# Scores of a retention layer in quarters of the TensorE array instead of row halves

## The chip, the core and the metric

The kernel runs on one core of a Trainium2 chip. TensorE does the matrix products, VectorE and ScalarE take their results out of PSUM and do the element-wise work, GpSimd one small scaling, and SyncE issues the DMA transfers. The metric is the device time of one execution in microseconds (us). A time that is compared is the median of several executions; the profile is of one more execution, whose own time is given beside it.

## The reference

A linear attention with decay is run over 768 tokens of 4 sequences with 8 heads of 64 dimensions; its output, seen as 3072 rows of 512, goes through a layer with a leaky ReLU of slope 0.01.

```python
# q, k, v: (4, 8, 768, 64) float32;  w_in: (512, 2048), w_out: (2048, 512)
gamma = 1.0 - 2.0 ** (-5.0 - np.arange(H))
for t in range(S):
    state = gamma * state + k[:, :, t] (outer) v[:, :, t]        # per batch and head, 64x64
    y[:, :, t] = (1 / np.sqrt(D)) * q[:, :, t] @ state
x = y.transpose(0, 2, 1, 3).reshape(B * S, H * D)                # (3072, 512)
h = x @ w_in
out = np.maximum(0.01 * h, h) @ w_out
```

All values are float32 in the result; the weights come in as 64-bit words and are turned into float32 on the chip.

## The kernel before

The 768 tokens are cut into 6 chunks (`c`) of 128 tokens (`C`). In each chunk every sequence (`b`, 4 of them) has its 8 heads held as 4 pairs (`a`, `HP = 4`) of two heads (`j`): a pair's 64 + 64 dimensions fill the 128 partitions. For one chunk and sequence the work is:

- `score` (lines 158 to 165): for each pair `a` and each head `j`, keys against queries. The 64 dimensions of head `j` lie on partitions 64j to 64j+63, so a product uses 64 rows of the array (row half `j`) and all 128 columns. The weights loaded are 128 key tokens, the moving operand 128 query tokens; the 128x128 result lies on all 128 partitions of PSUM. Results of head `j = 0` go to one bank, of `j = 1` to another (tile `ap`, two banks, two buffers under the tag `att`). Eight products.
- `masked` (line 169): VectorE multiplies the eight 128x128 blocks by a triangular mask, out of PSUM into the tile `am`, in one instruction.
- `reads` (line 183): the state of earlier chunks, 64x64 a head, against the queries. Weights of 64 rows (row half `j`) and 64 columns; the result goes to partitions 64i to 64i+63 (column half `i`), so that four products of a group lie in the four quarters of the array. Eight products, from chunk 1 on. Tile `yp`.
- `values` (line 192): masked scores times values: 128 rows, 64 columns (column half `i`), 128 moving columns; eight products onto the same tile `yp`.
- `state` (line 207): keys times values for the next chunk's state: 128 rows, 64 columns, 64 moving columns; eight products, from every chunk but the last.
- `taken` (lines 231 to 234): VectorE scales the result into `x` and renews the state.

The layer behind it takes `x` in chunks too. Its products are done in a scheme with seven block products instead of eight (`seven`, line 388, tiles A to D with the endings `_h` for the first and `_o` for the second matrix), or directly (`direct`, line 410, tile `d`) while the first weights are still being turned into float32; all these use the full array of 128x128 with 256 moving columns. One fp32 product is two records, a weight load and a matmul each, in the trace.

The order on each engine is the order in which the program is written; nothing reorders it. In the first stage (chunks 0 and 1, up to about 54 us) `score` is called for one sequence at a time, eight times, between steps of `direct` and, at the very start, between products that only keep the array busy (line 600). In the chunks 2 to 5 it is called for two sequences in a row, as the functions that `scored` returns: two such pairs of calls a chunk, placed after a given step of `seven` by the lists `at`, and the matching `read` (with `reads`, `values`, `state` and `taken`) three steps later. So in the span there are 24 calls of `score`: 8 alone and 8 pairs.

Of the kernel before, what the change touches and what calls it, by code (L numbers as in the profile page):

```python
# [23 lines left out]
def kernel(  # L24
# [35 lines left out]
    nc = tc.nc  # L60
# [94 lines left out]
    def two_banks(name):  # L155
        return psum.tile([128, 2, HP, C], FP32, tag="att", bufs=2, name=name)

    def score(c, b):

        x = heads[c, b][0]  # L160
        ps = scores[c, b] = two_banks(f"ap_{c}_{b}")
        for a in range(HP):
            for j in range(2):
                nc.tensor.matmul(ps[:, j, a, :], lhsT=x[ts(j, 64), 1, a, :],  # L164
                                 rhs=x[ts(j, 64), 0, a, :])

    def masked(c, b):
        am = work.tile([128, 2, HP, C], FP32, tag="am", bufs=2, name=f"am_{c}_{b}")
# [367 lines left out]
    def scored(c, b):  # L536
        def do():
            decay_v(c, b)
            score(c, b)
            masked(c, b)  # L540
        return do
# [48 lines left out]
    x, t = xs[0]  # L590
# [11 lines left out]

    keep_busy(7)
    score(0, 0)
    masked(0, 0)
    decay_v(0, 0)
    next_powers()
    keep_busy(8)
    score(0, 1)
    masked(0, 1)  # L610
    decay_v(0, 1)
# [209 lines left out]
```

## Time and profile before

| what | value |
|---|---|
| time, median of 4 executions | 672.12 us (672.08 to 672.36) |
| the profiled execution | 672.35 us |
| its span (first to last instruction) | 670.3 us |
| granted TensorE clock in it | 0.999 |
| products of `score` (line 164), matmul records | 304 + 48 + 32 = 384, by the tile that they read |
| the same as busy time | 20.9 + 3.5 + 2.3 us |
| products of `reads` (line 183), matmul records | 272 + 48 = 320; busy 9.5 + 1.8 us |
| VectorE's mask (line 169) | 24 instructions, 28.6 us busy |
| instruction queue | 32 packets, 0.52 MB |

A page of the profile gives busy time by engine, the span in 40 slices, the chain of work that ended last, and groups of instructions. Busy time of TensorE counts a record from its start to its modelled end, and records overlap, so it is not what a group costs; the start of the next record is the better measure. In the chain of waits every piece is the time from one release to the next, so its pieces add up to the span.

### The profile page before, as it was taken

The page shows a single profiled execution, that of the slowest core. Times are in us where ns is not written, and L with a number is a line of the kernel's source. Part 1 is how long each engine was busy: PE and PEld are TensorE (multiplying, and loading weights), DVE is VectorE, ACT ScalarE, POOL GpSimd, SP SyncE. Part 2 cuts the span into 40 slices and gives each one's busy share as a digit, 9 for nine tenths or more (in the row PEclk, how much of TensorE's full clock was granted, in tenths as well). Part 3 has the DMA queues.
Part 4 walks back from the last instruction along what each step waited for, and adds up shares of the span by engine and source line. Part 5 has one row for each costly group of instructions (what it writes and reads, how often), then busy time and mean ns, then how long its engine had stood idle before and what let it go on. Part 6 is the DMA issues. An engine that isn't in the chain of part 4 may idle for free.

```text
span 670.3 us, 9653 instructions
## 1 busy us (share of the span) xinstructions
PE 663.9 (99%) x4132; PEld 577.2 (86%) x4133; DVE 369.8 (55%) x563; ACT 174.2 (26%) x319; POOL 20.2 (3%) x23
## 2 busy tenths in 40 slices
PE   8999999999999999999999999999999999999997
PEld 4888888888888888888888888888888888888886
DVE  4778769889889675414642623553531444341342
ACT  4754456355252002210301210210211220221210
POOL 1000000000000111000000100100100000000000
PEclk9999999999999999999999999999999999999999
DMA  8922221222422553002002200301300000000001
GB/s 325 403 75 95 66 91 64 94 95 63 158 64 63 190 189 126 1 1 100 27 16 79 95 1 1 126 0 64 126 1 0 2 0 31 33 1 1 0 1 63
DMA packets 16025, 49.11 MB, mean 73 GB/s; under 512 B 1904, under 2 KB 2160, under 8 KB 15984
## 3 DMA queue, kind: packets, MB, share of 16 engines
q1 hardware_dynamic: 15984, 48.51, 20.6%
q8 instruction: 32, 0.52, 0.3%
q14 instruction: 9, 0.07, 0.0%
HBM read 42.21 MB, written 6.29 MB: 72 GB/s over the span
## 4 chain that ended last, share of the span: by engine, by line
PE 97%; DMA 1%; DVE 0%; issue 0%; SPq 0%; DVEq 0%
PE A_o L388 12%; PE B_o L388 12%; PE C_o L388 12%; PE B_h L388 12%; PE C_h L388 12%; PE A_h L388 11%; PE D_o L388 6%; PE D_h L388 6%; PE d L410 4%; PE ap L164 4%; PE yp L192 3%; PE yp L183 2%; PE yp L207 1%; DMA qk<-in_qk_dram 1%; PE sums L207 0%
## 5 line engine op out<-in xcount | busy, mean ns | idle before, releaser
L388 PE MATMUL A_h<-x,w 128*128 128x256 f32 x352 | 83.2, 379 | 0.0
L388 PEld LDWEIGHTS A_h<-x,w 128*128 128x128 f32 x352 | 66.9, 190 | 9.0
L388 PE MATMUL A_o<-g,w 128*128 128x256 f32 x288 | 68.0, 379 | 0.0
L423 ACT ACTIVATE g<-g 128x512 f32<-128x512 f32 x66 | 40.1, 630 | 87.0 <-DVE g L337 87.0
L388 PEld LDWEIGHTS A_o<-g,w 128*128 128x128 f32 x288 | 54.8, 190 | 7.4
L428 ACT COPY m<-A_h 128x512 f32<-128x512 f32 x22 | 12.8, 582 | 140.3 <-PE A_h L388 100.5
L337 DVE TENSOR_TENSOR m<-m,B_o 128x512 f32<-128x512 f32 x16 | 10.9, 684 | 65.9 <-PE B_o L388 65.9
L337 DVE TENSOR_TENSOR m<-m,B_h 128x512 f32<-128x512 f32 x22 | 15.1, 685 | 56.2 <-PE B_h L388 56.2
L231 DVE TENSOR_TENSOR x<-yp,dec 128x512 f32<-128x512 f32 x24 | 16.4, 687 | 47.7 <-PE yp L207 35.4
L388 PE MATMUL C_h<-t,w 128*128 128x256 f32 x176 | 42.2, 383 | 0.0
L388 PE MATMUL B_h<-x,w 128*128 128x256 f32 x176 | 42.2, 383 | 0.0
L388 PE MATMUL B_h<-t,w 128*128 128x256 f32 x176 | 41.6, 379 | 0.0
L388 PE MATMUL C_h<-x,w 128*128 128x256 f32 x176 | 41.6, 379 | 0.0
L388 PE MATMUL D_h<-t,w 128*128 128x256 f32 x176 | 41.6, 379 | 0.0
L340 DVE TENSOR_TENSOR gd<-g,gd 128x512 f32<-128x512 f32 x48 | 36.9, 769 | 1.8
L169 DVE TENSOR_TENSOR am<-ap,mask 128x1024 f32<-128x1024 f32 x24 | 28.6, 1220 | 16.2 <-PE ap L164 16.2
L388 PEld LDWEIGHTS C_h<-x,w 128*128 128x128 f32 x176 | 33.5, 190 | 4.5
L388 PEld LDWEIGHTS B_h<-t,w 128*128 128x128 f32 x176 | 33.5, 190 | 4.5
L388 PEld LDWEIGHTS D_h<-t,w 128*128 128x128 f32 x176 | 33.5, 190 | 4.5
L388 PEld LDWEIGHTS C_h<-t,w 128*128 128x128 f32 x176 | 33.0, 190 | 4.9
L388 PEld LDWEIGHTS B_h<-x,w 128*128 128x128 f32 x176 | 33.0, 190 | 4.8 <-issue 0.3
L388 PE MATMUL C_o<-g,w 128*128 128x256 f32 x144 | 34.0, 379 | 0.0
(109 smaller groups left out, 1046.2 us busy)
## 6 DMA issues: line engine op xcount, KB each, us to landing
raw<-in_weights_dram SPq DMA_DIRECT2D x31, 512.0 KB, 4.1
qk<-in_qk_dram SPq DMA_DIRECT2D x19, 512.0 KB, 4.1
kv<-in_kv_dram SPq DMA_DIRECT2D x17, 512.0 KB, 4.7
out_dram<-o SPq DMA_DIRECT2D x23, 256.0 KB, 2.1
in<-in_qk_dram SPq DMA_DIRECT2D x3, 512.0 KB, 7.3
in<-in_kv_dram SPq DMA_DIRECT2D x3, 512.0 KB, 7.8
kv<-in_kv_dram SPq DMA_DIRECT2D x4, 256.0 KB, 7.5
o_in<-in_qk_dram SPq DMA_DIRECT2D x2, 512.0 KB, 8.4
```

The lines of the kernel that those rows point to most:

```text
L164: nc.tensor.matmul(ps[:, j, a, :], lhsT=x[ts(j, 64), 1, a, :], rhs=x[ts(j, 64), 0, a, :])
L169: nc.vector.tensor_tensor(out=am.rearrange("p j a t -> p (j a) t"), in0=scores[c, b].rearrange("p j a t -> p (j a) t"), in1=mask.unsqueeze ...
L183: nc.tensor.matmul(ps[ts(i, 64), j, m, :], lhsT=st[b][ts(j, 64), a, :], rhs=x[ts(j, 64), 0, a, :], start=(m == 0), stop=False, skip_group_ ...
L192: nc.tensor.matmul(ps[ts(i, 64), j, m, :], lhsT=y[:, 1, 2 * a + j, :], rhs=am[:, j, a, :], start=(c == 0 and m == 0), stop=True, skip_grou ...
L207: nc.tensor.matmul(sp[ts(j, 64), a, :], lhsT=y[:, 0, 2 * a + j, :], rhs=y[:, 1, 2 * a + j, :], start=start, stop=True, skip_group_check=True)
L231: nc.vector.tensor_tensor(out=blocks, in0=ps[:, :, 0 : HP // 2, :], in1=gq, op=ALU.mult)
L337: nc.vector.tensor_tensor(out=out, in0=a, in1=b, op=ALU.add)
L340: nc.vector.tensor_tensor(out=out, in0=a, in1=b, op=ALU.subtract)
L388: nc.tensor.matmul(half, lhsT=block(w, sa)[:, k, ts(i, 128)], rhs=rhs[:, k, :], start=(first and (i == 0 or split) and n == 0 and k == 0), ...
L410: nc.tensor.matmul(banks[r][:, i, :], lhsT=block(2 * u, r + 2 * kh)[:, k, ts(i, 128)], rhs=x[:, 2 * kh + th, k, :], start=(step == 0 and i ...
L423: nc.scalar.activation(g[:, i], g[:, i], AF.Prelu, alpha=0.01)
L428: nc.scalar.copy(out=got["m1"], in_=ps)
```

## The change

Each product of `score` is made as two. The 128 key tokens that were loaded as one set of 128 columns are loaded as two sets of 64 columns (`u`); the results of the first set go to partitions 0 to 63 of PSUM, of the second to 64 to 127. The moving operand, the 128 query tokens of head `j`, is the same for both. The order is: for each pair `a`, for each column half `u`, for each row half `j`. The values that arrive in `ap` and their places are the same, and nothing else in the program is changed.

```diff
         for a in range(HP):
-            for j in range(2):
-                nc.tensor.matmul(ps[:, j, a, :], lhsT=x[ts(j, 64), 1, a, :],
-                                 rhs=x[ts(j, 64), 0, a, :])
+            for u in range(2):
+                for j in range(2):
+                    nc.tensor.matmul(ps[ts(u, 64), j, a, :], lhsT=x[ts(j, 64), 1, a, ts(u, 64)],
+                                     rhs=x[ts(j, 64), 0, a, :])
```

One call of `score` is 16 products instead of 8.

## The prediction

> **What bounds the kernel now.** I read the page's first part first, then its chain of waits, because the chain says where a saved microsecond can be collected.
>
> ```profile
> span 670.3 us, 9653 instructions
> PE 663.9 (99%) x4132; PEld 577.2 (86%) x4133; DVE 369.8 (55%) x563; ACT 174.2 (26%) x319; POOL 20.2 (3%) x23
> PEclk9999999999999999999999999999999999999999
> PE 97%; DMA 1%; DVE 0%; issue 0%; SPq 0%; DVEq 0%
> ```
>
> TensorE is busy 99% of the span at the full granted clock, and 97% of the chain that ended last is its own. No other engine or transfer holds it for long, so whatever a score block (the products of `score`, line 164) gains or loses on TensorE is gained or lost by the kernel, except before 14.85 us, where the chain runs over a transfer and VectorE. The second view is that chain in order of time, here between 0 and 63 us (start, length, what; x16 counts records, of which an fp32 product has two).
>
> ```profile
> 2.18 6.76 DMA qk<-in_qk_dram
> 8.98 1.19 PE ap L164 x16
> 13.52 1.29 DVE x L231 x2
> 16.85 1.09 PE ap L164 x16
> ...
> 36.62 1.03 PE yp L183 x32
> 37.66 1.90 PE yp L192 x32
> 39.55 0.93 PE yp L207 x32
> 40.49 1.92 PE d L410 x8
> 42.41 1.09 PE ap L164 x16
> ```
>
> Of the whole span the same view has eight pieces like this one, two blocks back to back:
>
> ```profile
> 302.66 1.99 PE ap L164 x32
> 304.64 1.92 PE C_h L388 x8
> ```
>
> The third view is the rows of the two tiles, with shapes (rows*columns of the array, then the moving operand):
>
> ```profile
> L164 PE MATMUL ap<-qk x304: 271/272/580, 4.5 to 521.8; 64*128 64x128 f32 x152
> L183 PE MATMUL yp<-qk,states x272: 268/269/322, 50.6 to 528.2; 64*64 64x128 f32 x136
> L192 PE MATMUL yp<-am,kv x304: 272/273/325, 10.9 to 530.1; 128*64 128x128 f32 x152
> ```
>
> The reader is to see that line 183, the state reads, already has the form the scores get: 64 rows by 64 columns, 128 moving columns, all four quarters. Its block of 16 products (32 records) takes 1.03 us; a score block of 8 products over full width (16 records) takes 1.09 us. The durations of about 270 ns overlap; the cost is the spacing of the starts.
>
> **The change, part by part.** Starts of single records, read from the trace, split these blocks. Score before: two records (one per row half) start together, and the next two follow 111.6 ns later; the first step is 101 ns longer, and from the last start to the next line's first is 201 ns. One block: 1091 ns; two back to back (16 steps): 1985 ns. State reads: four records start within 21 ns, the next four follow 109 ns later; the first step is 162 ns, the last start to the next line 199 ns; 1034 ns for 16 products.
>
> *A score block alone.* It goes from 8 products to 16 of exactly the state reads' shape, count and quarters: 1091 becomes 1034, -57 ns. There are eight such blocks, all before 46.5 us. The first, at 4.5 us, lies before the transfer that lands at 8.94 us and gains nothing. The second, at 8.98 us, releases VectorE's mask, which leads to the product at 14.85 us. The other six are on TensorE's own chain: at those places VectorE and ScalarE are ahead of TensorE by 0.2 us or more (the closest: the row of x that ends at 21.67 us ahead of a product at 21.91 us), and the saving so far is 0.17 us there. 7 x 57 = 399 ns. If that cover were gone, at most these 0.4 us would be lost.
>
> *Two blocks back to back.* From the third chunk on there are 8 such pairs. Each becomes 64 records, 16 steps of four: 1034 + 8 x 109 = 1906 against 1985, -79 ns; 8 x 79 = 632 ns.
>
> *Entering and leaving.* Entering costs the same for both forms (last start of the line before to the first of the block: 309 ns into line 164 and into line 183, where an unbroken stream has 216). Leaving a quarter form for the full array is not in the trace. Leaving it for 128*64 takes 199 ns, leaving 64*128 for the full array 201, leaving 128*64 with 64 moving columns for the full array 151: in each the last step plus about 92 ns. So I take 199, and 321 ns to the second full-array record, as now. Bounds: at best 103 ns, as where two lines of one form meet (192 to 207), at worst one more such 92 ns; per block -0.10 or +0.09 us, times 15.
>
> *The supply of instructions.* 24 x 8 = 192 more products are 384 more weight loads and 384 more matmul records, 768 on TensorE's stream. The instruction queue's row has 0.52 MB at 0.3% of the DMA engines for 9653 instructions; 8% more of that hides under transfers that are idle for most of the second half. How fast TensorE takes them is another matter: the state reads show 4 records per 109 ns for 32 records, not for the 64 of a pair. Nearest rows: 27 ns a record (the state reads' steps), and 40 ns, the longest dense stretch that the trace has (96 records of lines 183, 192 and 207 in 3.86 us). I take the 27 ns, since that row has the same form and no stall in it; the other end is a rival below.
>
> *The column halves.* In line 183 the two products on one row half read different moving columns; now they read the same ones. No row shows this. Below, nothing; above, no overlap of the two halves, the second rival. I take nothing: reading 512 bytes apart on the same partitions is free in line 183. The order also changes rows before columns, where line 183 changes columns first; its four start within 21 ns, so I give that no price.
>
> *VectorE, ScalarE, GpSimd, SyncE.* The same instructions in the same order. The mask (line 169) waits for the block's last product, which comes some 55 to 75 ns earlier; it waited 16.2 us in all, and its results are used at a later step of the same stage, so only the block at 8.98 us turns that into time. No wait is added.
>
> Sum: -0.40 - 0.63 = -1.0 us. Made against the profiled execution (span 670.3 us, 672.35 us in all, so 2.05 us around it) that is 671.3; against the median of the four runs, 672.12, it is **671.1 us**. With the early cover gone, 671.5.
>
> One rule speaks against the change. The state reads' weight loads of the second step start 53 ns after the first and under the running products: the first step lasts 162 ns, later ones 109, so they are hidden, although both quarters of a row half share rows. The Trainium skill, "TensorE: Matmul & The Clock Gate", section "Part 3: Packing small matmuls — row/col tiling", says weight loads overlap running matmuls only when the row groups differ. By that rule every step of four would be as long as the first, 8 x 162 + 92 = 1.39 us a block and 2.68 us a pair, and the sum +7.7 us; by the row it is the -1.0 us above. The measured steps contradict the rule for quarters, so I go by the row.
>
> **The rivals.** *(A) The pair outruns its supply.* Slower. Place: the second half of each of the 8 pairs, after the 32 records whose pace the trace shows. At 40 ns a record a pair takes 64 x 40.2 = 2.57 us, +0.59; 8 of them +4.7, less 0.4 from the single blocks: **676.4 us**. It decides from 31.8 ns a record on, where a pair costs (1985 + 50) / 64 and eats the single blocks' gain. For it: no stretch of 64 records here is that dense (lines 183 and 192 together take 2.83 us). Against it: the 40 ns are made by steps of two in line 192, and line 207's last records still come every 28 ns.
>
> The same page's table gives TensorE an engine queue of 64, and a state-read block is 64 instructions (loads counted); no run shows whether more than a queueful holds the pace.
>
> *(B) Only two quarters go at a time*, because both column halves read one moving operand or because of the order: the change doesn't do what it says. Steps of two: 16 x 111.6 + 200 = 1986 ns a block, 32 x 111.6 + 200 = 3771 a pair; 7 x 0.90 + 8 x 1.79 = +20.6: **692.7 us**. For it: no row has the shared operand. Against it: line 183's four starts within 21 ns.
>
> *(C) Leaving the quarters is cheap*: 103 instead of 199 ns, 15 times, -1.5 us more: **669.6 us**. For it: only that the pairing isn't in the trace. Against it: the 92 ns at every change of form in it.
>
> **How the numbers follow.** The forecast, -1.0 us, 0.66; A 0.12; B 0.12; C 0.10. The forecast's own range is 670.9 to 671.7 (all of the gain a little larger, or the early part gone and steps of 111 ns). C and B together are 0.22, so the range ends just above C's figure and at A's: 670.6 to 676.4. A change of 0.2% is 1.34 us, about what a measurement of this kernel can tell from none. Within it: nearly all of the forecast (0.62) and A just past its threshold (0.02), 0.64. Faster: C and the forecast's lower edge (0.04), 0.14. Slower: the rest of A (0.10) and B, 0.22.
>
> **What would show it.** Line 164 with 64*64 and 768 records; pieces of 1.03 us x32 and 1.91 us x64 in the chain; four starts, then 109 ns; 199 ns to the next line and 321 after; VectorE's rows as before. A pair above 2.03 us is A; four starts spread over two steps are B; a single block below 0.95 us is C. Wrong altogether if TensorE waits somewhere for VectorE that it didn't wait for before.

## The result and the profile after

The changed kernel takes 671.08 us (median of 42 runs, 670.37 to 671.66) against 672.10 us (60 runs, 671.46 to 672.56): a ratio of 0.9985 with a 95% interval of 0.9980 to 0.9989. That is 1.0 us less, 0.15%. The whole interval lies below 1, so the kernel is faster by a little: between 0.1 and 0.2%.

The page of the changed kernel (every line below 161 has moved down by one):

```profile
span 669.0 us, 10421 instructions
PE 662.7 (99%) x4516; PEld 575.2 (86%) x4517; DVE 367.8 (55%) x563; ACT 174.2 (26%) x319; POOL 22.8 (3%) x23
...
PEclk9999999999999999999999999999999999999999
...
q8 instruction: 35, 0.57, 0.4%
...
PE 98%; DMA 1%; DVE 0%; issue 0%; SPq 0%; DVEq 0%
```

TensorE has 384 more matmul records and as many more weight loads, and is still the whole chain. The instruction queue took three more packets. The rows of the tile `ap` show the new form, and in their last lines the mask's wait:

```profile
L165 PE MATMUL ap<-qk x608: 268/269/473, 4.5 to 520.4; 64*64 64x128 f32 x152
...
L165 PE MATMUL ap<-in x96: 268/269/321, 30.0 to 42.5; 64*64 64x128 f32 x96
...
L165 PE MATMUL ap<-o_in x64: 268/269/321, 16.4 to 21.2; 64*64 64x128 f32 x64
...
who waited for it (us, times):
  DVE am L170: 15.6, 12
```

The chain of waits in order of time (start, length, what), at the places shown before:

```profile
2.17 6.34 DMA qk<-in_qk_dram
...
8.55 1.15 PE ap L165 x32
...
13.10 1.29 DVE x L232 x2
...
16.43 1.04 PE ap L165 x32
...
35.97 1.03 PE yp L184 x32
37.01 1.90 PE yp L193 x32
38.90 0.93 PE yp L208 x32
39.84 1.92 PE d L411 x8
41.76 1.03 PE ap L165 x32
```

and, of the whole span, at one of the eight pairs:

```profile
301.66 1.91 PE ap L165 x64
303.57 1.93 PE C_h L389 x8
```

A score block now costs what a state-read block costs, 1.03 us, and a pair of them 1.91 us instead of 1.99. The pieces around them have kept their lengths. By the single starts, the 57 ns of a block are made of three things: its first step is 53 ns shorter (160 instead of 213), its six later steps are 14 ns shorter together, and its last start comes 13 ns later within its step, as four records take 20 ns to start where two took 7; the 2 or 3 ns left are in the leaving and in rounding.

The first line of the chain is another matter: in this execution the second transfer of queries and keys took 6.34 us instead of 6.76, and the first direct product stands 0.42 us earlier. That is a transfer's luck: the same kernel profiled once more (a1 below) had 6.92 us there, and in eight kernels profiled later (a1, e1, e2, e3, e7 to e10), which issue the same transfers there, the second score block began anywhere from 8.59 to 9.26 us. So the spans (670.3 and 669.0 us) differ by more than the medians do.

The second block's own saving does not reach the first direct product. From that block's start to that product's it is 5.88 us before and 5.88 after. The chain's piece for the block is shorter (1.19 to 1.15 us), and VectorE's first instruction on a piece of weights behind the mask is longer by as much. Two lines of the timeline before,

```profile
9.76 2.04 POOL L147 TENSOR_TENSOR kv<-kv,dec 128x512 f32<-128x512 f32 x2 [8.32 <-DMA kv<-in_kv_dram]
11.33 0.75 DVE L329 TENSOR_SCALAR w<-raw 128x512 uint32<-128x512 uint32 x1
```

and after:

```profile
9.33 2.04 POOL L147 TENSOR_TENSOR kv<-kv,dec 128x512 f32<-128x512 f32 x2 [7.90 <-DMA kv<-in_kv_dram]
10.87 0.79 DVE L330 TENSOR_SCALAR w<-raw 128x512 uint32<-128x512 uint32 x1
```

VectorE's instruction takes 0.75 and 0.79 us here, against 0.41 and 0.42 us the next time, when GpSimd is idle (14.72 and 14.29 us), and it ends 0.28 us after GpSimd has scaled the values, however early it began (0.28 to 0.29 us in ten of the thirteen profiles). In these ten (all but e4, e5 and e6, whose blocks are much longer) the first direct product starts 5.10 to 5.11 us after GpSimd's first scaling does, whatever form the second score block has: in e3 that block starts 0.04 us later than in the changed kernel's first profile, GpSimd 0.20 and the first direct product 0.21 us later. GpSimd starts when its transfer lands. So GpSimd and its transfer set the time there, and not the score block. Why VectorE's instruction is held until then the traces do not show.

For these reasons the experiments below are read by two figures from the trace: the length of a block, from its first record's start to the start of the next line's first record, and the *ledger*, from the first direct product (14.85 us before, 14.43 us after) to the last matmul's start. In the kernel before the ledger is 651.750 us; after the change it is 650.785, 0.965 us less.

### The profile page after: what moved, and what is told of

It reads as the page before. It is cut to its first block, busy times and chain, and to the rows that moved or that the text cites. A ratio compares the mean times of both kernels' runs of the same rounds, so it can differ in the third digit from the quotient of the medians.

```text
span 669.0 us, 10421 instructions
## 1 busy us (share of the span) xinstructions
PE 662.7 (99%) x4516; PEld 575.2 (86%) x4517; DVE 367.8 (55%) x563; ACT 174.2 (26%) x319; POOL 22.8 (3%) x23
## 4 chain that ended last, share of the span: by engine, by line
PE 98%; DMA 1%; DVE 0%; issue 0%; SPq 0%; DVEq 0%
PE A_o L389 12%; PE B_o L389 12%; PE C_o L389 12%; PE C_h L389 12%; PE B_h L389 12%; PE A_h L389 11%; PE D_o L389 6%; PE D_h L389 6%; PE d L411 4%; PE ap L165 3%; PE yp L193 3%; PE yp L184 2%; PE yp L208 1%; DMA qk<-in_qk_dram 1%; PE sums L208 0%
## 5 line engine op out<-in xcount | busy, mean ns | idle before, releaser
L147 POOL TENSOR_TENSOR kv<-kv,dec 128x512 f32<-128x512 f32 x18 | 22.3, 1243 | 460.8 <-DMA kv<-in_kv_dram 251.4
L170 DVE TENSOR_TENSOR am<-ap,mask 128x1024 f32<-128x1024 f32 x24 | 28.6, 1220 | 15.6 <-PE ap L165 15.6
L341 DVE TENSOR_TENSOR gd<-g,gd 128x512 f32<-128x512 f32 x48 | 34.0, 709 | 1.8
```

Of the source, the lines that this page charges most:

```text
L147: engine.tensor_tensor(out=v, in0=v, in1=gk.unsqueeze(2).to_broadcast([128, H, D]), op=ALU.mult)
L170: nc.vector.tensor_tensor(out=am.rearrange("p j a t -> p (j a) t"), in0=scores[c, b].rearrange("p j a t -> p (j a) t"), in1=mask.unsqueeze ...
L341: nc.vector.tensor_tensor(out=out, in0=a, in1=b, op=ALU.subtract)
```

## The experiments

| kernel | one block, ns | a pair, ns | ledger against the kernel before, us | the same from the blocks, us |
|---|---|---|---|---|
| before | 1091 | 1985 | 0 | |
| changed, first and second profile | 1034, 1034 | 1908, 1907 | -0.965, -0.964 | 6 x -57 + 8 x -77.5 = -0.962 |
| e1, pairs alone | 1092 | 1908 | -0.616 | 8 x -77.5 = -0.620 |
| e2, single blocks alone | 1034 | 1985 | -0.342 | 6 x -57 = -0.342 |
| e3, columns first | 1034 | 1908 | -0.962 | 6 x -57 + 8 x -77 = -0.96 |
| e4, sorted by quarter | 2494 | 4468 | +28.275 | 6 x 1403 + 8 x 2483 = +28.28 |
| e5, form changing inside | 1602 | 3203 | +12.807 | 6 x 511 + 8 x 1218 = +12.81 |
| e6, everything twice | 1907 | 3654 | +18.251 | 6 x 816 + 8 x 1669 = +18.25 |
| e7, eighths | 1086 | 1959 | -0.238 | 6 x -5 + 8 x -26 = -0.24 |
| e9, two of a quarter in a row | 1098 | 2058 | +0.620 | 6 x 7 + 8 x 73 = +0.63 |

The last two columns agree within 0.02 us in every row: after the first direct product nothing but the length of the blocks moves the time, even when the blocks become 28 us longer in all.

**Where the microsecond is: the pairs (e1) and the single blocks (e2).** Two kernels with quarters in one of the two places; this edit and those that follow are against the changed kernel:

```diff
         for a in range(HP):
-            for u in range(2):
+            if c > 1:
+                for u in range(2):
+                    for j in range(2):
+                        nc.tensor.matmul(ps[ts(u, 64), j, a, :], lhsT=x[ts(j, 64), 1, a, ts(u, 64)],
+                                         rhs=x[ts(j, 64), 0, a, :])
+            else:
                 for j in range(2):
-                    nc.tensor.matmul(ps[ts(u, 64), j, a, :], lhsT=x[ts(j, 64), 1, a, ts(u, 64)],
+                    nc.tensor.matmul(ps[:, j, a, :], lhsT=x[ts(j, 64), 1, a, :],
                                      rhs=x[ts(j, 64), 0, a, :])
```

In e2 the condition is `c < 2` in place of `c > 1`.

> Quarters in the eight pairs of score blocks alone (chunks 2 to 5); the eight single blocks stay in row halves. Theory (a block is worth what its steps say, wherever it stands): pairs of 1908 ns, singles of 1091 ns, 8 x 78 = 0.62 us below the kernel before, 671.5 us. Rival (what the pairs save is lost again at a later wait): 672.1 us.

> Quarters in the eight single blocks alone (chunks 0 and 1). Theory: singles of 1034 ns, pairs of 1985 ns, 6 x 57 ns on TensorE's own chain and up to 57 ns for the second block, so 0.34 to 0.40 us below the kernel before, 671.7 us. Rival (the first stage is set by transfers and VectorE, so nothing is gained there): 672.1 us.

Measured: 671.81 us (ratio 0.9993, 0.9984 to 1.0002) and 671.92 us (0.9993, 0.9984 to 1.0001), beside 672.38 us for the kernel before on the same chip. The intervals alone can't tell either from no change; the ledgers can, -0.616 and -0.342 us, and they add up to -0.958, beside the -0.965 of both. The rivals fall: nothing is lost again at a later wait, and the six single blocks behind the first direct product count in full.

**The order of the quarters (e3).**

```diff
-            for u in range(2):
-                for j in range(2):
+            for j in range(2):
+                for u in range(2):
```

> The changed kernel with the order of the four quarters turned: the two column halves of a row half come first, as in line 183. Theory (the order of four neighbours does not matter): blocks of 1034 and pairs of 1908 ns, 671.1 us. Rival (rows before columns is a better or a worse order): steps of four other than 109 ns; each ns is worth 8 x 7 + 16 x 8 = 184 ns of the whole.

Measured: 671.40 us (0.9985, 0.9976 to 0.9994), the median block and pair the same to the nanosecond. The order of four neighbours doesn't matter.

**A long stretch (e6).** Each block is computed twice over.

```diff
+        for _ in range(2):
             for a in range(HP):
                 for u in range(2):
                     for j in range(2):
...
```

(The lines inside the new loop are indented further and otherwise as they were.)

> Each score block is computed twice over, into the same place: 32 products a block, 128 records in a row in a pair. Theory (the pace of 109 ns for four records holds as long as one likes): blocks of 1906 ns and pairs of 3653 ns, 7 x 0.87 + 8 x 1.745 = 20 us over the changed kernel, 691 us, up to 1 us more where the mask comes too late for its products in the first stage. Rival (the instructions of a long stretch run short): steps above 109 ns from some record on; at the 40 ns a record of the longest stretch in the kernel before, 5.1 us a pair, 703 us.

Measured: 691.49 us in one run, beside 672.28 for the kernel before. A pair in the chain of waits of this kernel:

```profile
369.71 3.65 PE ap L166 x128
```

The starts of its 128 records go in steps of four, 109 ns apart, to the last (160, 269, 378 ... 3326, 3435 ns). The theory predicted 3653 ns and it is 3654. So rival (A) of the prediction, that a long stretch outruns its instructions, is wrong up to 128 records (256 instructions with the weight loads), twice what a pair needs. The 0.9 us by which the run exceeds the ledger lie before the first direct product (15.75 instead of 14.85 us), where longer blocks delay the mask.

**Does it need neighbours in different quarters (e4, e9)?** First all four products of a quarter in a row, then two:

```diff
-        for a in range(HP):
-            for u in range(2):
-                for j in range(2):
+        for u in range(2):
+            for j in range(2):
+                for a in range(HP):
```

```diff
-        for a in range(HP):
-            for u in range(2):
-                for j in range(2):
+        for m in range(HP // 2):
+            for u in range(2):
+                for j in range(2):
+                    for a in (2 * m, 2 * m + 1):
```

> The changed kernel with its products sorted by quarter: the four products of one quarter in a row, then the next quarter's, so that neighbours in the program cannot go together. Theory (each quarter has a queue of its own, filled far enough ahead): still eight steps of 109 ns a block, 671.1 us. Rival (only neighbours overlap): one quarter at a time, 32 records of 107 ns, 3.4 us a block and 6.9 us a pair, 7 x 2.4 + 8 x 4.9 = 56 us more, 727 us. A look-ahead of some length lies between.

> The changed kernel with two products of one quarter in a row before the next quarter's. Sorting by whole quarters let a quarter begin when the one before it started its fifth record of eight. Theory (a quarter takes four records, one running and three waiting, and only the fifth holds up what is behind it): two products are four records, so nothing is held up, blocks of 1034 ns, steps of 109 ns, 671.1 us. Rival (whatever is sorted overlaps less): between 1034 and the 2494 ns of the full sorting, with quarters two or three at a time.

Sorted by quarter the kernel takes 702.84 us (one run), and both extremes are wrong. The timeline of TensorE around its last pair (start, length, line, shape, records):

```profile
547.05 1.03 PE L389 MATMUL B_h<-t,w 128*128 128x256 f32 x4
548.00 4.54 PE L165 MATMUL ap<-qk 64*64 64x128 f32 x64
552.47 1.99 PE L389 MATMUL C_h<-t,w 128*128 128x256 f32 x8
```

From 548.00 to 552.47 the pair takes 4.47 us. The single starts say how (the trace does not name a record's quarter; which is which is read from the order of the program and the spacing): the first quarter's go at 0, 160, 269, 378 and 487 ns alone; at 493 ns, with the fifth of its eight records, the second quarter begins; the third follows at 987 ns, with the fifth of the second. Never more than two go together. The second quarter's first record thus starts ahead of the first quarter's sixth, at 597 ns, though it stands behind it in the program: by this reading TensorE's records do not start strictly in the order written, unlike what the description of the kernel before says. One block is three such delays of 493 ns, then the last quarter's eight records (815 ns) and 199 ns for leaving: 2493, measured 2494.

I read from it that a quarter takes four records, one running and three waiting, and that a fifth holds up what is behind it. The kernel with two products (four records) of a quarter in a row was made to test that, and it bears it out only in part. Its first 20 records do go in steps of four at 109 ns, as expected (0, 14, 27, 40; 160, 174, 187, 200; ... 487, 501, 515, 528). Then, at 597 ns, one quarter is on time and the other three follow only 57 to 83 ns after it, and in a pair this grows until the four go one after the other within a step. A pair takes 2058 ns instead of 1908, and the kernel 673.17 us in its one run. A limit of four records in each quarter explains the start and not the slip; what causes the slip is open.

**The price of a change of form (e5).**

```diff
         for a in range(HP):
-            for u in range(2):
+            if a % 2 == 1:
+                for u in range(2):
+                    for j in range(2):
+                        nc.tensor.matmul(ps[ts(u, 64), j, a, :], lhsT=x[ts(j, 64), 1, a, ts(u, 64)],
+                                         rhs=x[ts(j, 64), 0, a, :])
+            else:
                 for j in range(2):
-                    nc.tensor.matmul(ps[ts(u, 64), j, a, :], lhsT=x[ts(j, 64), 1, a, ts(u, 64)],
+                    nc.tensor.matmul(ps[:, j, a, :], lhsT=x[ts(j, 64), 1, a, :],
                                      rhs=x[ts(j, 64), 0, a, :])
```

> The head pairs 0 and 2 in row halves, 1 and 3 in quarters, so that the form changes three times more in a block. Theory (each change of form empties the array and shows the first load: last start to the next form about 200 ns, first step 213 or 162 ns): 2 x (414 + 361) = 1550 ns a block and 3100 ns a pair, 7 x 0.52 + 8 x 1.19 = 13 us over the changed kernel, 684 us. Rival (both forms use 64 rows, so a change between them costs nothing): 1.08 us a block, 672 us.

Measured: 687.10 us in one run. The timeline of its last pair:

```profile
533.57 0.49 PE L170 MATMUL ap<-qk 64*128 64x128 f32 x4
533.99 0.45 PE L166 MATMUL ap<-qk 64*64 64x128 f32 x8
534.37 0.49 PE L170 MATMUL ap<-qk 64*128 64x128 f32 x4
534.79 0.45 PE L166 MATMUL ap<-qk 64*64 64x128 f32 x8
```

The starts of the groups are 0.42 and 0.38 us apart. The last start before a change and the first after it are 199 to 202 ns apart in both directions, and the first step after it is long again. A block costs 1602 ns, 540 above the mean of the two pure forms (1063): three changes more, 180 ns each. Both forms use 64 rows, and that saves nothing: the rival falls. The expected 1550 ns were 3% low, and the ledger is 13.8 us over the changed kernel's against 13. The run as a whole is 3 us above the expected 684; most of that lies before the ledger, where the first direct product starts 2.4 us later than in the changed kernel's profile.

**Eighths (e7).**

```diff
-            for u in range(2):
+            for u in range(4):
                 for j in range(2):
-                    nc.tensor.matmul(ps[ts(u, 64), j, a, :], lhsT=x[ts(j, 64), 1, a, ts(u, 64)],
+                    nc.tensor.matmul(ps[ts(u, 32), j, a, :], lhsT=x[ts(j, 64), 1, a, ts(u, 32)],
```

> Each product of the kernel before as four of 32 columns: eight at a time, 32 products a block. Theory (the array sets the step, the first load of a block is what shrinks: 101 ns over a step for 128 columns, 53 for 64, so about 27 for 32): blocks of 1007 ns, pairs of 1880 ns, 0.4 us below the changed kernel, 670.7 us. Rival (instructions cannot follow: a product needs the 27 ns that a step of four gives it): 64 x 27.3 = 1.75 us a block and 3.5 us a pair, 7 x 0.66 + 8 x 1.5 = 16.6 us over the kernel before, 689 us.

Measured: 672.04 us (0.9996, 0.9987 to 1.0005), ledger -0.238: neither figure. The rival is wrong by far; eight records do start in a step of 109 ns, 128 in 1.96 us:

```profile
518.79 1.03 PE L389 MATMUL B_h<-t,w 128*128 128x256 f32 x4
519.74 2.03 PE L165 MATMUL ap<-qk 64*32 64x128 f32 x128
521.70 1.99 PE L389 MATMUL C_h<-t,w 128*128 128x256 f32 x8
```

And the excess of the first step shrinks with the columns that are loaded, as the theory says: the first step is 133 ns, 24 above the others (53 for 64 columns, 101 for 128). What the theory left out is the time between the first and the last of a step. Eight starts take some 46 ns in the first steps; from the 37th record on they come mostly 17 ns apart instead of 7, and a step's eight take 100 ns. In quarters it is 20 ns. A block is then 133 + 6 x 109 + 100 + 199 = 1086, as measured; a quarter block 160 + 6 x 109 + 20 + 200 = 1034. The shorter load saves 27 ns and the later last start costs 80.

**Fewer changes of form (a1, e8, e10).** If a change costs what e5 shows, blocks are better put side by side. In chunk 1 the scores of the sequences 2 and 3 have eight direct records between them; in e8 they are back to back. In e10 those of the sequences 0 and 1 are too, at the later one's place. The edit of e8, then what e10 has besides:

```diff
     scored_later(2)
+    scored_later(3)
     steps = direct(1, 0, x1, parts[1][1], 0)
     next(steps)
-    scored_later(3)
```

```diff
-    scored_later(0)
     decay_v(1, 1, nc.scalar)
     next(steps)
+    scored_later(0)
     scored_later(1)
```

> The changed kernel itself once more, to stand beside the next one on the same chip: 1.0 us below the kernel before, blocks of 1034 and pairs of 1908 ns.

> The changed kernel with the scores of the sequences 2 and 3 of chunk 1 back to back, where a step of the direct products lay between them. Theory (what is left to save is the changes of form: leaving a block and entering it again costs 92 + 53 + 15 ns on the block's side and 93 + 105 on the full array's): 0.36 us below the changed kernel, 670.7 us, in the trace one pair of 1908 ns near 41.7 us and a run of 24 direct records without a break. Rival (the second block waits for its PSUM buffer, which VectorE leaves about 0.3 us after the first one starts, or its mask comes too late): no gain, 671.1 us.

> Besides the sequences 2 and 3, the sequences 0 and 1 of chunk 1 have their scores back to back, at the place of sequence 1's, one step of the direct products later than sequence 0's before. Theory (two breaks less): 2 x 0.36 = 0.72 us below the changed kernel from the first direct product on, 670.4 us. Rival (sequence 0's mask comes 3 us later on VectorE, and what it does next, the mantissas of the next weights, reaches TensorE too late): TensorE waits before the direct products that follow lines 184 to 208, and up to the 0.36 us of this step is lost, 670.8 to 671.1 us.

The changed kernel, once more: 671.22 us (0.9981, 0.9972 to 0.9990). e8: 671.10 us (0.9982, 0.9973 to 0.9990). e10, on another occasion: 670.72 us (0.9972, 0.9963 to 0.9982). Beside these stand 672.42, and for e10 672.55 us, of the kernel before. The chain of waits of e8:

```profile
40.53 1.92 PE d L411 x8
42.45 1.91 PE ap L165 x64
44.36 5.38 PE d L411 x24
49.74 1.03 PE yp L184 x32
```

and of the changed kernel at the same place:

```profile
39.84 1.92 PE d L411 x8
41.76 1.03 PE ap L165 x32
42.79 1.92 PE d L411 x8
44.72 1.03 PE ap L165 x32
45.75 3.65 PE d L411 x16
49.40 1.04 PE yp L184 x32
```

From the end of the first line to the start of the last it is 7.29 us instead of 7.64. The ledger of e8 is 0.359 us below the changed kernel's, where 0.36 was expected; no wait of TensorE for a PSUM buffer or for a mask appears. The medians differ by 0.12 us only and the intervals overlap, so the time alone doesn't show the gain.

e10's ledger is 0.520 us below, not 0.72. The second merging gives 0.161 us, and TensorE waits nowhere new: behind the first direct product no two of its starts lie more than 321 ns apart, as in the kernel before. The estimate was wrong in a simpler way than the rival has it: sequence 0's block did not lie between two stretches of direct products but between the state sums and one, where the form changes in any case. Taking it away leaves the change from the sums to the direct products, so that only 2 x 1034 - 1907 = 161 ns of the block's own are saved. By its ledger, 1.484 us below the kernel before's where the changed kernel's is 0.965 below, e10 is the fastest version here. Its ratio, taken on another occasion, has an interval that just overlaps the changed kernel's, so the times alone don't set the two apart.

## Why the prediction was right

- *TensorE is the whole chain.* Confirmed behind the first direct product: in nine kernels the ledger follows the block lengths within 0.02 us.
- *A single block, 1091 to 1034 ns.* Measured 1033 to 1035 for the six that count. The price came from a row with the same shape, count and quarters, so it was read and not estimated.
- *The second block, 57 ns through VectorE.* Wrong, though too small to matter. From its start to the first direct product it is 5.88 us before and after: the saving is used up in VectorE's next instruction, which ends 0.28 us after GpSimd's work however early it began; the prediction left GpSimd out of this path. The first stage's gain is the 6 x 57 = 342 ns that e2 shows, not 7 x 57 = 399.
- *A pair, 1985 to 1906 ns.* Measured 1906 to 1909. The steps of 109 ns hold (e6: to 128 records), so rival (A) is excluded. (The spacing of line 207's last records, which the prediction sets against (A), is 29 ns in the trace and not 28; nothing hangs on it.)
- *Leaving the quarters, 199 ns, and 321 to the second full-array record.* Measured 198 to 200 and 319 to 321. Rival (C), 103 ns, is excluded. The some 90 ns above the last step come with every change of form that the runs have, between the two forms of 64 rows too (e5).
- *The shared moving operand and the order of the quarters at no price.* Right: four starts within 20 ns, steps of 109 ns, and e3 has the same. Rival (B) is excluded for this order. Its fear wasn't empty: with the same products sorted by quarter (e4) only two go at a time.
- *The other engines.* Right: the mask waits 15.6 instead of 16.2 us, VectorE's and ScalarE's counts are as before.
- *The rule of the Trainium skill* ("TensorE: Matmul & The Clock Gate", section "Part 3: Packing small matmuls — row/col tiling") that weight loads overlap running matmuls only in other row groups: here two quarters of each row half load while the same half computes (in a single block of the changed kernel the second four loads start 54 to 73 ns after the first matmul does, and by the profile that one runs to 321 ns), and steps stay at 109 ns. By the rule it would have been +7.7 us, the prediction's estimate; measured is -1.0.

The sum was -1.03 us and the medians differ by 1.02. Part of so close an agreement is luck: without the second block the sum is -0.97, which is what the ledger has (0.965), and the interval of the ratio allows anything from 0.7 to 1.3 us; single runs of one kernel spread over 1.1 to 1.3 us.

## What to carry to other kernels

When products are cut into smaller array forms, look for a line of the same kernel that already runs in that form: the spacing of its starts prices the change, its busy time doesn't. Where two row halves already fill the array, quarters gain little in each step (109 against 111.6 ns) and some 50 ns in the first step of a stretch, while a change of form avoided is worth 160 to 180 ns, so put stretches of one form side by side. Let neighbours in the program go to different quarters, and don't cut so small that the starts of one step spread by more than the shorter first step saves. And where the chain of waits runs over several engines, as before the first direct product here, a shorter piece need not shorten the whole: look for what else that stretch waits for.

## What the runs showed of the hardware that had not been expected

- Products in the same quarter hold up those behind them: with eight records of a quarter in a row the next quarter begins only with the fifth (493 ns after the first), and a block takes 2494 instead of 1034 ns. With four records in a row it begins at once, but from the 22nd record on the quarters drift apart (2058 instead of 1908 ns a pair). The second isn't explained.
- Eight parts of 64 rows by 32 columns go at a time in steps of 109 ns, over 128 records, but from the 37th record on the starts within a step come some 17 ns apart instead of 7. What sets the 17 ns is open.
- A change between 64*128 and 64*64 costs as much as one to the full array, about 200 ns from the last start to the first, though the rows are divided alike.
- VectorE's instruction on a piece of weights takes 0.75 and 0.79 us while GpSimd scales the values, and 0.41 and 0.42 us while GpSimd is idle; it ends 0.28 us after GpSimd does. What couples them is open.
